# Float32 score operands over 128 partitions, batch 0's values loaded once, and a turn table in place of a planner

## The chip, the core and the metric

The kernel runs on one core of a Trainium2 chip. The metric is the device time of one execution in microseconds (us). A core has five engines that work side by side, each through its own list of instructions in a fixed order: TensorE (PE, matrix products; its weight loads are listed apart as PEld), VectorE (DVE), ScalarE (ACT), GpSimd (POOL) and SyncE (SP), which here issues every DMA. A transfer that SP issues is carried by the core's 16 DMA engines.

## The reference

Attention with a decay for 8 batches and 8 heads over 576 positions of width 64, and behind it a two-layer feed-forward net with the activation h·cos(h):

```python
scores = scale * np.matmul(q, k.transpose(0, 1, 3, 2))
cum = np.cumsum(np.log(np.clip(f, 0.0001, 1.0)), axis=-1)
scores = np.where(causal, -1000000000.0, scores + cum[:, :, :, None] - cum[:, :, None, :])
attn = np.exp(scores - scores.max(-1)); attn = attn / (attn.sum(-1) + 1e-09)
x = np.matmul(attn, v)            # -> 4608 tokens x 512
h = x @ w_in                      # 512 -> 2048
out = (h * np.cos(h)) @ w_out     # 2048 -> 512
```

## The kernel before

**Tiles and stages.** A unit of attention is a pair of heads, n = 0 to 31 (four to a batch); a unit of the net is half a batch's tokens, u = 0 to 15, of 320 or 256 tokens. For each pair the scores of a 128-row block come out of one or two matmuls (`mm`, into PSUM tiles pa1 and pa2), DVE adds the causal mask and takes the row maximum, ACT takes the exponential. `gemm1` (L1058) is the first layer: 12 matmuls for each 128 rows of h, float16 high and low parts; then DVE and ACT form h·cos(h) and split it into the two parts of g. `gemm2` (L1105) is the second layer.

**Three kinds of score operands.** Pairs 0 to 3 go through `attention32` (L764) and pairs 4 to 7 through `attention` with float32 operands too (NQ = 8): 16 heads. Their q and k lie in a tile "q32" of the ring `g` (pairs 0 to 3) or `stage` (pairs 4 to 7), filled by `load32` (L753): 64 partitions of q and k from DRAM (L759) and four partitions of decay sums from the DRAM tile `cum_d` (L760), so that a score matmul contracts over 68 partitions (L818, L973). From pair 8 on, scores are two matmuls of rounded parts (L975, L976).

**Weights.** W1 and W2 arrive as 64-bit words, 512 KB for each of 32 chunks (`stage`, L602; DMA at L627). DVE turns each chunk into float32 in three passes (L617, L621, L625), ACT takes a bound (L636). When all chunks of a column group are there, a scale is formed, and each chunk is split into float16 high (ACT, L646) and low (DVE, L653). W1's column group must be split before its `gemm1`, all of W2 before the first `gemm2`.

**Values.** `prep_vscale` (L705) loads the four value tiles of a batch into `stage` (L709) for a bound; the attention units load the same tiles again, into ring `v2` (L769 and L905).

**Buffers.** A ring is a set of buffers used in turn: `BUFS` gives their number (g 8, h 3, stage 2, v2 2). A tile waits until the last user of the tile that held its buffer is done.

**What sets the order.** All operations are recorded in a `Plan`, and `order` (L359) decides for each engine the order in which they are written. It runs a forward model of the engines with assumed costs, ranks by due times, runs it again, and then adds a hand-kept table `SHIFT` of time offsets. The model has a clock for TensorE (`Clock`, L222), and where it sees TensorE wait in the first 200 us (`FILL`) it writes filler matmuls on constant data ahead of the operation (`pads`, emitted at L1186), whose results are thrown away. Once written, each engine's order is fixed: an instruction that waits holds up all that stands behind it on its engine, SP's DMA issues included. Some operations have an alternative engine (`alt`): copies out of PSUM (ACT or DVE), the subtraction that makes g's low part (DVE L1101, or POOL L1102), the two subtractions behind the rounded q and k (L921, L922).

Of the kernel before, what the change touches and what calls it, by code (L numbers as in the profile page):

```python
# [24 lines left out]
P = 128  # L25
# [18 lines left out]
HOLDV, HOLDW, HOLDR, HOLDX = 0.0, 0.0, 25.0, 25.  # L44
NHP = 3
N32, NQ = 4, 8
ROUNDS = 2
AHEAD = 15
EARLY = 2
FILL, PAD = 200, 448  # L50
SWITCH = 6.0
TWO_PI = 2.0 * np.pi
NEG = -8.0e9
BUFS = dict(xs=1, stage=2, v2=2, vv=2, pt3=3, pt2=2, xh0=8, xl0=8, xh1=8, xl1=8, h=3, r=1, g=8, ot=1,
            pa2=1, pa1=3, hp=3, dg=1)

SHIFT = {
# [158 lines left out]
DMQ, DMC = int(1.35 * 360e3), int(0.5 * 360e3)  # L216
PADG, PADE, PE0 = 0.3, 0.0, 2.5
VACT = 2
T_DGE, T_DMA0, T_DMA1, DMA_BW, T_TABLE = 0.5, 0.65, 0.9, 360e3, 1.28


class Clock:  # L222
# [994 lines left out]
```

## Time and profile before

| | |
|---|---|
| time, 3 runs | median 1072.54 us (1072.24 to 1073.82) |
| the profiled execution's own time | 1073.1 us |
| its span, first to last instruction | 1071.4 us |
| mean granted TensorE clock | 0.992 |
| busy: PE, DVE, ACT, POOL | 1050.1, 819.7, 832.2, 155.3 us |
| filler matmuls | 158, 34.5 us of PE's busy time |
| DMA | 146.37 MB, mean 137 GB/s |

How to read it: "busy" of an engine is the union of its instructions' spans; filler matmuls count as PE's work in it. "Idle before" or "waited" is the time in which an engine had nothing running, put down to what ended it. "PEclk" is the share of full speed that TensorE's clock was granted. "DMA share" is the mean busy share of the 16 DMA engines, and a row of windows gives, for a stretch of the span, each engine's busy time (with its number of instructions), the clock, the DMA share and the rate.

### The profile page before, as it was taken

The numbers are of one execution on the slowest core, as the hardware profiler recorded it, in microseconds if no ns is written. First come the engines' busy times: TensorE is split into PE (matmuls) and PEld (weight loads), VectorE is DVE, ScalarE is ACT, GpSimd is POOL, SyncE is SP. The second block draws the span as 40 slices with busy tenths as digits, with TensorE's granted clock in tenths as the row PEclk, the third lists the DMA queues.
The fourth block names the chain that finished last, engine by engine and source line by source line (L and its number), as shares of the span: only waits on it lengthen the run. The fifth ranks groups of instructions, "written<-read, shape, count | busy, mean of one in ns | idle before, by whom it ended". The sixth has DMA issues, their size and how long they took to land. (4 is left out here: it accounts for less than half of the span.)

```text
span 1071.4 us, 23498 instructions
## 1 busy us (share of the span) xinstructions
PE 1050.1 (98%) x8975; PEld 841.6 (79%) x8975; DVE 819.7 (77%) x1801; ACT 832.2 (78%) x1739; POOL 155.3 (14%) x271
## 2 busy tenths in 40 slices
PE   8999999899999999999999999999999999999998
PEld 4778776688778887788778877778778877788787
DVE  6989999677887979678886879778776868671613
ACT  4758989588887989788888979887877978762522
POOL 1000000121121220221112211211211222000000
PEclk9999999799999999999999999999999999999999
DMA  8893463667767566647766667765776564430000
GB/s 267 309 284 109 99 135 102 126 162 158 180 152 147 139 142 167 149 101 159 182 154 144 127 148 167 169 129 130 178 144 144 134 142 75 85 59 21 7 20 20
DMA packets 256280, 146.37 MB, mean 137 GB/s; under 512 B 223337, under 2 KB 231529, under 8 KB 256169
## 3 DMA queue, kind: packets, MB, share of 16 engines
q1 hardware_dynamic: 256168, 144.88, 58.4%
q8 instruction: 70, 1.15, 0.5%
q14 instruction: 42, 0.34, 0.1%
HBM read 72.11 MB, written 10.62 MB: 77 GB/s over the span
## 5 line engine op out<-in xcount | busy, mean ns | idle before, releaser
L1118 PE MATMUL hp<-g,W2s 128*128 128x256 f16 (+1 forms) x3072 | 390.9, 287 | 0.6 <-DVE W2s L653 0.4
L1072 PE MATMUL hp<-xh,W1s 128*128 128x256 f16 (+1 forms) x2048 | 380.4, 286 | 1.1 <-ACT h L1078 1.1
L1118 PEld LDWEIGHTS <-W2s 128*128 128x128 f16 x3072 | 297.9, 98 | 78.0 <-issue 0.8
L1072 PEld LDWEIGHTS <-W1s 128*128 128x128 f16 x3072 | 295.9, 98 | 78.6 <-issue 1.7
L1072 PE MATMUL hp<-xl,W1s 128*128 128x256 f16 (+1 forms) x1024 | 292.6, 286 | 0.0
L1013 DVE SCALAR_TENSOR_TENSOR PS<-pa,ri,PS 128x576 f16<-128x576 f32 (+2 forms) x280 | 140.7, 544 | 32.1 <-ACT PS L1009 31.3
L992 ACT ACTIVATE pa<-pa,nb 128x576 f32<-128x576 f32 (+2 forms) x280 | 141.1, 506 | 19.8 <-DVE nb L987 18.6
L987 DVE CUSTOM_DVE_ANT_0 pa<-pa,mask 128x576 f32<-128x576 f32 (+2 forms) x280 | 131.5, 513 | 31.8 <-PE pa L976 26.1
L1009 ACT ACTIVATE PS<-pa,ri 128x576 f16<-128x576 f32 (+2 forms) x280 | 134.1, 545 | 15.0 <-DMA pt<-PS 9.7
L1078 ACT ACTIVATE h<-hp 128x320 f32<-128x320 f32 (+1 forms) x256 | 101.3, 416 | 36.6 <-PE hp L1072 36.0
L1093 DVE TENSOR_TENSOR h<-h,r 128x1280 f32<-128x1280 f32 (+1 forms) x64 | 89.1, 1392 | 41.4 <-ACT r L1091 41.2
L997 POOL TENSOR_SCALAR ri<-L 128x1 f32<-128x1 f32 (+1 forms) x168 | 46.8, 279 | 410.4 <-ACT pa L992 404.9
L921 POOL TENSOR_TENSOR QK<-stage,QK 64x576 fp32r<-64x576 f32 x46 | 77.3, 1680 | 170.5 <-issue 116.4
L1091 ACT ACTIVATE r<-r,halfpi,m_inv 128x1280 f32<-128x1280 f32 (+1 forms) x64 | 86.2, 1347 | 18.8 <-DVE r L1089 18.3
L1101 DVE TENSOR_TENSOR g<-h,g 128x1280 f16<-128x1280 f32 (+1 forms) x62 | 84.2, 1358 | 14.1 <-ACT g L1100 13.7
L1087 DVE TENSOR_SCALAR r<-h,m_a 128x1280 int32<-128x1280 f32 (+1 forms) x64 | 56.8, 888 | 49.3 <-ACT h L1078 48.3
L1089 DVE SCALAR_TENSOR_TENSOR r<-r,m_b,h 128x1280 f32<-128x1280 int32 (+1 forms) x64 | 91.3, 1426 | 0.7
L975 PE MATMUL pa<-QK 128*128 128x288 f32 (+4 forms) x288 | 90.3, 330 | 1.5 <-DVE PS L1013 1.5
L1100 ACT CAST g<-h 128x1280 f16<-128x1280 f32 (+1 forms) x64 | 74.2, 1159 | 15.1 <-DVE h L1093 14.9
L1124 ACT ACTIVATE ot<-hp,m_o 128x320 f32<-128x320 f32 (+1 forms) x64 | 32.3, 504 | 65.9 <-PE hp L1118 50.4
L1042 PEld LDWEIGHTS <-vv 128*64 128x64 f16 x1512 | 69.4, 111 | 16.9 <-issue 14.2
L1042 PE MATMUL pa<-pt,vv 128*64 128x256 f16 (+2 forms) x1512 | 78.8, 256 | 3.7 <-DMA pt<-PS 3.4
(118 smaller groups left out, 1166.7 us busy)
## 6 DMA issues: line engine op xcount, KB each, us to landing
stage<-in_dram SPq DMA_DIRECT2D x48, 576.0 KB
stage<-in_dram SPq DMA_DIRECT2D x32, 320.0 KB
v<-in_dram SPq DMA_DIRECT2D x32, 320.0 KB
g<-in_dram SPq DMA_DIRECT2D x16, 512.0 KB
h<-in_dram SPq DMA_DIRECT2D x16, 512.0 KB
QC<-QK SPq DMA_DIRECT2D x48, 144.0 KB
out_dram<-ot SPq DMA_DIRECT2D x32, 160.0 KB
out_dram<-ot SPq DMA_DIRECT2D x32, 128.0 KB
```

The source lines that it names most:

```text
L975: T.matmul(c, hi[:, 0, isl], hi[:, 1, d], start=True, stop=False)
L987: op("DVE", c_dve(w) + 0.008, lambda view=view, ib=ib, o=o, w=w, mk=mk, c=c: V.tensor_tensor_reduce(out=view(ib, o, w), in0=view(ib, o, w) ...
L992: op("ACT", c_act(w, True, 2), lambda view=view, ib=ib, o=o, w=w, c=c: A.activation(view(ib, o, w), view(ib, o, w), AF.Exp, bias=nb.get()[ ...
L1009: op("ACT", c_act(w, True, 1), lambda view=view, ib=ib, o=o, w=w, c=c, out_=out_: A.activation(out_(0), view(ib, o, w), AF.Copy, scale=ri. ...
L1013: op("DVE", c_dve(w) + 0.06, lambda view=view, ib=ib, o=o, w=w, c=c, out_=out_: V.scalar_tensor_tensor(out_(1), view(ib, o, w), ri.get()[: ...
L1042: T.matmul(d, vv.get()[:, jb, hd, kv], m, start=first and x == 0, stop=last and x == 2)
L1072: T.matmul(hp.get()[:, 0:w_], WS_[1][:, at(1, 4 * c + cb), w, fs], x.get(), start=(n == 0), stop=(n == 11))
L1078: op("ACT", c_act(w_, True), lambda hp=hp, k=k: A.activation(h.get()[:, k, 0:w_], hp.get()[:, 0:w_], AF.Copy, scale=float(2.0 ** -24)), re ...
L1089: op("DVE", c_dve(N) + 0.045, lambda: V.scalar_tensor_tensor(fl(r), fl(r).bitcast(I32), b1.get()[:, c:c + 1], fl(h), op0=ALU.mult, op1=ALU ...
L1091: op("ACT", c_act(N, aps=2), lambda: A.activation(fl(r), fl(r), AF.Sin, scale=inv.get()[:, c:c + 1], bias=halfpi), reads=[inv], writes=[r] ...
L1093: op("DVE", c_dve(N), lambda: V.tensor_tensor(fl(h), fl(h), fl(r), op=ALU.mult), reads=[r], writes=hk, prio=pr)
L1118: T.matmul(po.get()[:, 0:w_], WS_[2][:, at(2, 4 * c + k), w, msl], gh.get()[:, i, k, 0:w_], start=(n == 0), stop=(n == 47))
```

## The change

- **Operands.** A second input `qk2` holds q and k of the first 16 heads with 60 rows of zeros below the 64 of data: 124 rows. `load32` fills partitions 4 to 127 from it and partitions 0 to 3 with the decay sums, and the score matmuls of these heads contract over 128 partitions instead of 68. `qkT` keeps the other batches alone.
- **Values.** `load_v` keeps one tile per pair, and `prep_vscale(0)` reads that tile (ACT, junk output into ring `ot`): the values of batch 0 are loaded once. Ring v2 has 4 buffers instead of 2, ring g 7 instead of 8.
- **Order.** `rank`, `backward`, `shift` and `SHIFT` go. `TURN` lists all operations by number, and that place is the only key by which the model picks; `SWAP` names the operations that take their alternative engine. By the count of instructions in the order, POOL gets 36 of the 64 g subtractions (2 before), ACT 31 of 40 copies out of PSUM (25 before), and there are 115 filler matmuls (158 before), of which 75 stand ahead of the first score matmul (91 before) and 15 ahead of the first `gemm2` (none before). The model's constants change (DMA rate, clock thresholds, `FILL` 240), which counts only through the fillers.

```diff
-BUFS = dict(xs=1, stage=2, v2=2, vv=2, pt3=3, pt2=2, xh0=8, xl0=8, xh1=8, xl1=8, h=3, r=1, g=8, ot=1,
+BUFS = dict(xs=1, stage=2, v2=4, vv=2, pt3=3, pt2=2, xh0=8, xl0=8, xh1=8, xl1=8, h=3, r=1, g=7, ot=1,
...
+TURN = (
+    0, 6, 54, 30, 29, 1, 3, 74, 16, 7, 4, 8, 349, 59, 55, 56, 9, 57, 10, 58, 11, 12, 13, 75, 79, 76, 77, 18, 17, 78, 351, 350, 64, 60, 61,
...
     def order(self):
-        self.rank()
...
+        for k, i in enumerate(TURN):
+            o = self.ops[i]
+            o.due = k
+            if i in SWAP:
+                o.eng, o.cost, o.fn = o.alt[:3]
+        return self.forward()
...
-                    o = min(q, key=lambda x: (x.due - x.first + (switch if x.table not in (None, table) else 0.0), x.id))
+                    o = min(q, key=lambda x: x.due)
...
+    def load_v(n, pr):
+        if n not in V2:
+            b, p = divmod(n, NP)
+            v2 = V2[n] = ring("v2", [P, 5, P], F32)
+            op("SP", T_DGE, lambda: dma(v2.get(), vp[b, p].rearrange("p (j c) -> p j c", c=P)), writes=[v2], prio=pr, size=VSZ)
+        return V2[n]
...
+            if b == 0:
+                v2, jk = load_v(p, pr), ring("junk", [P, 640], BF16, tag="ot")
+                op("ACT", c_act(640, aps=1), lambda v2=v2, jk=jk, p=p: A.activation(
+                    jk.get(), v2.get().rearrange("p j c -> p (j c)"), AF.Square, accum_out=mx.get()[:, p:p + 1]),
+                   reads=[v2], writes=[mx.part(p), jk], prio=pr)
+                continue
...
-        op("POOL", 0.23, lambda: G.memset(q.get()[0:68, 0, 0:64], 0.0), writes=[q.part(0)], prio=pr - 1)
-        op("SP", T_DGE, lambda: dma(q.get()[0:64, :, ks], qkT[b, p, hd, 0:64]), writes=[q.part(1)], prio=pr - 1, size=DMQ)
-        op("SP", T_DGE, lambda: dma(q.get()[64:68, :, ks], cum_d[b * H + 2 * p + hd]),
+        op("POOL", 0.23, lambda: G.memset(q.get()[:, 0, 0:64], 0.0), writes=[q.part(0)], prio=pr - 1)
+        op("SP", T_DGE, lambda: dma(q.get()[4:P, :, ks], qk2[b, p, hd]), writes=[q.part(1)], prio=pr - 1, size=DMQ)
+        op("SP", T_DGE, lambda: dma(q.get()[0:4, :, ks], cum_d[b * H + 2 * p + hd]),
...
-                            T.matmul(c, qf.get()[0:68, 0, isl], qf.get()[0:68, 1, 64 + d.start:64 + d.stop], start=True, stop=True)
+                            T.matmul(c, qf.get()[:, 0, isl], qf.get()[:, 1, 64 + d.start:64 + d.stop], start=True, stop=True)
...
+    qk2 = np.zeros((nb, NP, 2, P - 4, 2, S), qk.dtype)
+    qk2[:, :, :, 0:D] = qk[:nb]
+    qkT = np.ascontiguousarray(np.concatenate([qk[nb:], qk[nb:]], axis=3))
```

SP's list, around the loads of q and k that follow the third head's (tiles g_582, g_586 and two of stage before; g_300 and two of stage now). L759 and L760 before are L774 and L775 now (q and k, decay sums); L627 is a chunk of weights (g_ for W2, h_ for W1). Before:

```order
L769 DMA v2_578<-in_1_dram 128x640
L760 DMA g_582<-cum_d_105 4x2x576
L759 DMA g_582<-in_0_dram 64x2x576
L627 DMA g_604<-in_4_dram 128x1024
L760 DMA stage_599<-cum_d_105 4x2x576
L759 DMA g_586<-in_0_dram 64x2x576
L627 DMA h_621<-in_3_dram 128x1024
```

Now:

```order
L627 DMA h_327<-in_4_dram 128x1024
L774 DMA g_300<-in_0_dram 124x2x576
L774 DMA stage_319<-in_0_dram 124x2x576
L774 DMA stage_309<-in_0_dram 124x2x576
L930 DMA QC0_82<-cum_d_105 4x2x576
L775 DMA stage_309<-cum_d_105 4x2x576
L627 DMA g_388<-in_5_dram 128x1024
L627 DMA h_397<-in_4_dram 128x1024
```

Three loads of 124 rows now stand one behind the other, two of them for pair 4, ahead of the twelfth weight chunk (g_388); before, weight chunks stood between them.

DVE's list, around the first mask of the sixth head (pa2_887 before; pa2_781 now, from tile g_678). L826 before is L839 now (mask and maximum), L617 to L625 the passes over a weight chunk, L894 before and L907 now the low part of x. Before:

```order
L617 TENSOR_SCALAR W1s_98<-h_817 128x512
L566 TENSOR_SCALAR dg_893<-eye_73,vm1_623 128x128
L894 SCALAR_TENSOR_TENSOR xl1_895<-hp_876,vs_471,xh1_890 128x256
L621 SCALAR_TENSOR_TENSOR W1s_98<-h_817,W1s_98 128x512
L826 ISA pa2_887,nb_730<-pa2_887,mask_66 128x2x288
L826 ISA nb_730 128x1
```

Now:

```order
L621 SCALAR_TENSOR_TENSOR W2s_99<-g_613,W2s_99 128x512
L907 SCALAR_TENSOR_TENSOR xl0_793<-hp_753,vs_351,xh0_770 128x320
L625 SCALAR_TENSOR_TENSOR W2s_99<-g_613,W2s_99 128x512
L839 ISA pa2_781,nb_652<-pa2_781,mask_66 128x2x288
L839 ISA nb_652 128x1
```

The mask stands behind fewer chunks of weights than before: three chunks' second and third passes have moved behind it.

More of the change, by code (lines that the diff above doesn't have):

```diff
@@ L43 @@
 LEAD = 2.5
-HOLDV, HOLDW, HOLDR, HOLDX = 0.0, 0.0, 25.0, 25.
+HOLDV, HOLDW, HOLDR = 0.0, 0.0, 25.0
 NHP = 3
 N32, NQ = 4, 8
-ROUNDS = 2
-AHEAD = 15
 EARLY = 2
-FILL, PAD = 200, 448
-SWITCH = 6.0
+FILL, PAD = 240, 448
 TWO_PI = 2.0 * np.pi
 NEG = -8.0e9
-BUFS = dict(xs=1, stage=2, v2=2, vv=2, pt3=3, pt2=2, xh0=8, xl0=8, xh1=8, xl1=8, h=3, r=1, g=8, ot=1,
+BUFS = dict(xs=1, stage=2, v2=4, vv=2, pt3=3, pt2=2, xh0=8, xl0=8, xh1=8, xl1=8, h=3, r=1, g=7, ot=1,
             pa2=1, pa1=3, hp=3, dg=1)
-SHIFT = {
[122 rows of a table removed]
-}
+TURN = (
[183 rows of a table added]
+)
+SWAP = {36, 43, 51, 50, 53, 116, 147, 473, 474, 569, 597, 663, 1005, 1004, 1206, 1207, 701, 1290, 1289, 1054, 1332, 1333, 1372, 1373, 1092,
[4 rows of a table added]
 class Buf:
@@ L207 @@
 class Op:
-    __slots__ = ("eng", "cost", "size", "table", "fn", "prio", "deps", "succ", "n", "ready", "id", "t", "alt", "due", "port", "first", "moving", "bank", "fill", "end", "pads", "hold")
+    __slots__ = ("eng", "cost", "size", "table", "fn", "prio", "deps", "succ", "n", "ready", "id", "t", "alt", "due", "port", "moving", "bank", "fill", "end", "pads", "hold")
 LAT = {("ACT", "ACT"): 0.034, ("ACT", "DVE"): 0.131, ("ACT", "PE"): 0.17, ("ACT", "POOL"): 0.18, ("ACT", "SP"): 0.13,
@@ L215 @@
 SHARED = {"DVE": "POOL", "POOL": "DVE"}
-DMQ, DMC = int(1.35 * 360e3), int(0.5 * 360e3)
+DMQ, DMC, VSZ = 8 * 124 * 576, int(0.4 * 410e3), 4 * P * 5 * P
 PADG, PADE, PE0 = 0.3, 0.0, 2.5
 VACT = 2
-T_DGE, T_DMA0, T_DMA1, DMA_BW, T_TABLE = 0.5, 0.65, 0.9, 360e3, 1.28
+T_DGE, T_DMA0, T_DMA1, DMA_BW, T_TABLE = 0.5, 0.65, 0.9, 410e3, 1.28
 class Clock:
-    W, HIGH, LOW, SLOW = 3.413, 0.49, 0.36, 2.0
+    W, HIGH, LOW, SLOW = 3.413, 0.36, 0.4, 2.0
     def __init__(self):
@@ L231, in close @@
         u = self.busy / self.W
-        self.warm = u > self.HIGH or (self.warm and u > self.LOW)
+        self.warm = u > (self.LOW if self.warm else self.HIGH)
         self.k, self.busy = self.k + 1, 0.0
@@ L254, in pad @@
             e = min(b, (self.k + 1) * self.W)
-            self.busy += (e - a) * (0.9 if self.warm else 0.5)
+            self.busy += (e - a) * (0.9 if self.warm else 0.45)
             n += (e - a) / ((1.0 if self.warm else 2.0) * (PAD / 2400 + 0.003))
@@ L264, in __init__ @@
     def __init__(self):
-        self.ops, self.rings, self.first = [], {}, 0.0
+        self.ops, self.rings = [], {}
     def ring(self, name, make):
@@ L278, in op @@
         o.eng, o.cost, o.size, o.table, o.fn, o.prio, o.alt, o.id = eng, cost, size, table, fn, prio, alt, len(self.ops)
-        o.port, o.first, o.moving, o.fill, o.pads, o.hold = port, self.first, moving, fill, 0, hold
+        o.port, o.moving, o.fill, o.pads, o.hold = port, moving, fill, 0, hold
         o.bank = []
@@ L310, in op @@
         return o
-    def rank(self):
-        t = 0.0
-        for o in self.ops:
-            o.due = 1e9
-        for o in sorted((o for o in self.ops if o.eng == "PE"), key=lambda o: (o.prio, o.id)):
-            o.due = t
-            t += o.cost
-        for o in reversed(self.ops):
-            c = T_DMA0 + o.size / DMA_BW + T_DMA1 if o.eng == "SP" else o.cost + 0.15
-            for x in o.succ:
-                o.due = min(o.due, x.due - c)
-    def backward(self, end):
-        free, avail, future, n = {}, {}, [], {}
-        late = {}
-        for o in self.ops:
-            free.setdefault(o.eng, 0.0)
-            avail.setdefault(o.eng, [])
-            n[o.id], late[o.id] = len(o.succ), 0.0
-            if not o.succ:
-                heapq.heappush(future, (0.0, o.id, o))
-        t, left = 0.0, len(self.ops)
-        while left:
-            while future and future[0][0] <= t + 1e-9:
-                o = heapq.heappop(future)[2]
-                heapq.heappush(avail[o.eng], (-end[o.id], o.id, o))
-            nxt = []
-            for e, q in avail.items():
-                if q and free[e] <= t + 1e-9:
-                    o = heapq.heappop(q)[2]
-                    left -= 1
-                    free[e] = t + o.cost
-                    stop = t + (T_DMA0 + o.cost + o.size / DMA_BW if e == "SP" else o.cost)
-                    o.due = -stop
-                    for d in o.deps:
-                        late[d.id] = max(late[d.id], stop + (T_DMA1 if d.eng == "SP" else LAT[d.eng, e]))
-                        n[d.id] -= 1
-                        if not n[d.id]:
-                            heapq.heappush(future, (late[d.id], d.id, d))
-                if q:
-                    nxt.append(free[e])
-            if future:
-                nxt.append(future[0][0])
-            t = max(t, min(nxt, default=t))
@@ L359, in order @@
-    def order(self):
-        self.rank()
-        base = [(o.eng, o.cost, o.fn) for o in self.ops]
-        for k in range(ROUNDS):
-            if k:
-                self.backward(end)
-            for o, x in zip(self.ops, base):
-                o.eng, o.cost, o.fn = x
-            out, end = self.forward()
-        self.shift()
-        return self.forward(0.0)[0]
-    def shift(self):
-        group = {}
-        for o in self.ops:
-            k = group.setdefault((o.fn.__code__.co_firstlineno, o.prio), o.id)
-            o.due, o.alt = o.t + o.first + SHIFT.get(k, 0.0), None
@@ L378, in forward @@
-    def forward(self, switch=SWITCH):
-        free, avail, future, out, ends = {}, {}, [], [], {}
+    def order(self):
+        for k, i in enumerate(TURN):
[4 more added lines that the diff above has]
+        return self.forward()
+    def forward(self):
+        free, avail, future, out = {}, {}, [], []
         for o in self.ops:
@@ L392, in forward @@
                 _, _, o = heapq.heappop(future)
-                if o.alt:
-                    def done(e, c):
-                        return max(t, free[e]) + c + sum(x.cost for x in avail[e] if x.due - x.first <= o.due - o.first)
-                    if done(o.alt[0], o.alt[1]) <= done(o.eng, o.cost) + o.alt[3]:
-                        o.eng, o.cost, o.fn = o.alt[:3]
                 avail[o.eng].append(o)
@@ L427, in forward @@
                     if e == "SP":
-                        dma_free = max(dma_free, t + min(o.cost, 0.625) + T_DMA0) + o.size / (DMA_BW if t > 10.0 else 0.6 * DMA_BW)
+                        dma_free = max(dma_free, t + min(o.cost, 0.625) + T_DMA0) + o.size / (DMA_BW if t > 5.0 else 0.6 * DMA_BW)
                         end = dma_free
@@ L432, in forward @@
                     span = max(span, end)
-                    ends[o.id] = o.end = end
+                    o.end = end
                     for s in o.succ:
@@ L445, in forward @@
         self.span = span
-        return out, ends
+        return out
 def c_dve(n, fast=False, k=1):
@@ L473, in fox_moe_kernel @@
 @with_exitstack
-def fox_moe_kernel(ctx: ExitStack, tc: tile.TileContext, qkT, vp, fT, w1, w2, out):
+def fox_moe_kernel(ctx: ExitStack, tc: tile.TileContext, qk2, qkT, vp, fT, w1, w2, out):
     nc = tc.nc
@@ L703, in fox_moe_kernel @@
     vs, ms = {}, {}
+    V2 = {}
+    def load_v(n, pr):
[4 more added lines that the diff above has]
+        return V2[n]
     def prep_vscale(b, pr):
@@ L767, in attention32 @@
         pr = float(n)
-        v2 = ring("v2", [P, 5, P], F32)
-        op("SP", T_DGE, lambda: dma(v2.get(), vp[b, p].rearrange("p (j c) -> p j c", c=P)), writes=[v2], prio=pr - 0.9,
-           size=4 * P * 5 * P, hold=HOLDX)
+        v2 = load_v(n, pr - 0.9)
         ks = slice(64, 64 + S)
@@ L790, in mm @@
                         o += 1
-            op("PE", 0.11 * nb_, mm, reads=reads, writes=[pm], prio=pr + 0.2, moving=0.48, fill=lambda: pm.get()[:, 0:PAD])
+            op("PE", 0.11 * nb_, mm, reads=reads, writes=[pm], prio=pr + 0.2, moving=0.9, fill=lambda: pm.get()[:, 0:PAD])
             o = 0
@@ L817, in mm @@
                         for c, d in ((d_[:, 0], slice(0, hf)), (d_[:, 1], slice(hf, S))) if big else ((d_, slice(0, w)),):
-                            T.matmul(c, qf.get()[0:68, 0, isl], qf.get()[0:68, 1, 64 + d.start:64 + d.stop], start=True, stop=True)
-                op("PE", 2 * c_mm4(S // 2) if big else sum(c_mm4(w) for _, _, w in blocks), mm, reads=xb, writes=[tb], prio=pr, fill=lambda tile_=tile_, big=big: tile_.get()[:, 0, 0:PAD] if big else tile_.get()[:, 0:PAD])
+                            T.matmul(c, qf.get()[:, 0, isl], qf.get()[:, 1, 64 + d.start:64 + d.stop], start=True, stop=True)
+                op("PE", 2 * c_mm4(S // 2) if big else sum(c_mm4(w) for _, _, w in blocks), mm, reads=xb, writes=[tb], prio=pr, moving=0.64, fill=lambda tile_=tile_, big=big: tile_.get()[:, 0, 0:PAD] if big else tile_.get()[:, 0:PAD])
                 for ib, o, w in blocks:
@@ L888, in turn_x @@
                     T.transpose(pm.get()[:, k * P:k * P + P], xs.get()[:, k].rearrange("p h d -> p (h d)"), eyef)
-            op("PE", 0.11 * m, turn_x, reads=[xs], writes=[pm], prio=pr + 0.6, moving=0.48, fill=lambda pm=pm: pm.get()[:, 0:PAD])
+            op("PE", 0.11 * m, turn_x, reads=[xs], writes=[pm], prio=pr + 0.6, moving=0.9, fill=lambda pm=pm: pm.get()[:, 0:PAD])
             xh, xl = ring(f"xh{half}", [P, w], F16), ring(f"xl{half}", [P, w], F16)
@@ L903, in attention @@
         pr = float(n)
-        v2 = ring("v2", [P, 5, P], F32)
-        op("SP", T_DGE, lambda: dma(v2.get(), vp[b, p].rearrange("p (j c) -> p j c", c=P)), writes=[v2], prio=pr - 0.9,
-           size=4 * P * 5 * P)
+        v2 = load_v(n, pr - 0.9)
         sets = [0, 0] if n < NQ else [next(turn) % NSET for hd in range(2)]
@@ L914, in prep @@
             qk = ring("stage", [P, 2, S], F32)
-            op("SP", T_DGE, lambda: dma(qk.get(), qkT[b, p, hd]), writes=[qk], prio=pr - 1, size=8 * P * S)
+            op("SP", T_DGE, lambda: dma(qk.get(), qkT[b - NQ // NP, p, hd]), writes=[qk], prio=pr - 1, size=8 * P * S)
             op("ACT", c_act(2 * S), lambda: A.copy(hi[:, :, ks], qk.get()), reads=[qk], writes=[x["hi"]], prio=pr)
@@ L972, in mm @@
                             if q32:
-                                T.matmul(c, q32.get()[0:68, 0, isl], q32.get()[0:68, 1, d], start=True, stop=True)
+                                T.matmul(c, q32.get()[:, 0, isl], q32.get()[:, 1, d], start=True, stop=True)
                                 continue
@@ L978, in attention @@
                 x2 = c_mm4 if q32 else lambda w: 2 * c_mmr(w)
-                op("PE", 2 * x2(S // 2) if big else sum(x2(w) for _, _, w in blocks), mm, reads=xb, writes=[tb], prio=pr, fill=lambda tile_=tile_, big=big: tile_.get()[:, 0, 0:PAD] if big else tile_.get()[:, 0:PAD])
+                op("PE", 2 * x2(S // 2) if big else sum(x2(w) for _, _, w in blocks), mm, reads=xb, writes=[tb], prio=pr, moving=0.64 if n < NQ else 1.0, fill=lambda tile_=tile_, big=big: tile_.get()[:, 0, 0:PAD] if big else tile_.get()[:, 0:PAD])
                 c0 = col
@@ L1146, in adv @@
         if n < len(gens):
-            pl_.first = AHEAD
             next(gens[n], None)
-            pl_.first = 0.0
     decay()
@@ L1195 @@
     qk = np.stack([x.transpose(0, 1, 3, 2).reshape(B, NP, 2, D, S) for x in (q, k)], axis=4)
-    qkT = np.ascontiguousarray(np.concatenate([qk, qk], axis=3))
+    nb = NQ // NP
+    qk2 = np.zeros((nb, NP, 2, P - 4, 2, S), qk.dtype)
+    qk2[:, :, :, 0:D] = qk[:nb]
+    qkT = np.ascontiguousarray(np.concatenate([qk[nb:], qk[nb:]], axis=3))
     vs = np.zeros((B, NP, 5 * P, P), v.dtype)
@@ L1202 @@
     ws = [w.view(np.int64) if w.dtype.itemsize == 8 else w for w in ws]
-    arrays = [qkT, vp, fT, *ws]
+    arrays = [qk2, qkT, vp, fT, *ws]
     nc = _bacc.Bacc("TRN2", target_bir_lowering=False, num_devices=1, dynamic_dma_scratch_size=1024)
```

308 rows, old and new, of tables (SHIFT, SWAP, TURN) are left out of this document.

## The prediction

> **What bounds the kernel now.** First the page's totals, then the windows by stage: up to the first `gemm1`, to the first weight chunk of W2 needed, to the first `gemm2`, and the rest.
>
> ```profile
> span 1071.4 us, 23498 instructions
> PE 1050.1 (98%) x8975; PEld 841.6 (79%) x8975; DVE 819.7 (77%) x1801; ACT 832.2 (78%) x1739; POOL 155.3 (14%) x271
> 0.00:114.30 114.30, 106.32 (x665) 79.13 (x666) 100.65 (x292) 77.15 (x220) 8.17 (x43) 0.99 0.74 229
> 114.30:166.80 52.50, 51.05 (x410) 38.18 (x409) 51.14 (x128) 48.09 (x102) 2.56 (x10) 1.00 0.54 115
> 166.80:204.30 37.50, 32.58 (x210) 21.95 (x208) 32.92 (x70) 29.39 (x61) 3.08 (x10) 0.82 0.54 133
> 204.30:1071.40 867.10, 860.13 (x7698) 702.36 (x7695) 634.99 (x1315) 677.58 (x1358) 141.45 (x209) 1.00 0.58 126
> ```
>
> Each row gives the stretch, its length, busy time (and number) of PE, PEld, DVE, ACT and POOL, the clock, the DMA share and GB/s. From 204.3 us on PE is busy 860.1 of 867.1 us: that stage is PE's own work, and the change does not touch it except through POOL. Time can be won or lost ahead of it. There "PE busy" misleads, since it holds the fillers (the second answer below counts them alone), and DVE has to be read in two halves:
>
> ```profile
> 0.00:114.30 114.30, 34.46 (x158) 15.93 (x158) 0.99 0.74 229
> 20.00:79.90 59.90, 55.18 (x344) 41.71 (x342) 55.18 (x159) 42.08 (x122) 1.00 (x7) 0.97 0.97 296
> 79.90:115.30 35.40, 34.43 (x245) 29.31 (x244) 34.88 (x116) 28.52 (x83) 2.31 (x12) 1.00 0.34 101
> ```
>
> Between 20 and 80 us the DMA engines are full (0.97); from 80 us to the first `gemm1` DVE is (34.88 of 35.40), with the DMA at 0.34. So the chain is: loads up to the sixth head's operands, then DVE, then PE. Its marks on the timeline (start, length, operation):
>
> ```profile
> 2.29 18.89 PE L1186 MATMUL pa<-mask,ones 128*128 128x448 bf16 x91 [2.29 <-POOL ones L497]
> 21.02 2.97 PE L818 MATMUL pa<-g 68*128 68x288 f32 x12
> 77.39 3.03 PE L818 MATMUL pa<-g 68*128 68x288 f32 x12
> 79.04 0.76 DVE L826 CUSTOM_DVE_ANT_0 pa<-pa,mask 128x576 f32<-128x576 f32 x1
> 114.29 0.43 PE L1072 MATMUL hp<-xh,W1s 128*128 128x320 f16 x2
> 114.95 0.48 DVE L894 SCALAR_TENSOR_TENSOR xl<-hp,vs,xh 128x256 f16<-128x256 f32 x1
> ```
>
> The sixth head's scores start at 77.39, its first mask at 79.04; from there DVE takes 35.9 us to its last low part of x ahead of `gemm1` (114.95), and `gemm1` starts at 114.29.
>
> **The new loads.** A load of q and k had 64 rows of partitions and now has 124. What that does depends on how many of the 16 engines carry it, and the trace can be asked, since every transfer ends with one 4-byte packet from each engine that took part. The first row below is a window with nothing but a 4-row load, the second one with only a 64-row copy, the third the whole span.
>
> ```profile
> DMA packets 12, 0.02 MB, mean 18 GB/s; under 512 B 4, under 2 KB 4, under 8 KB 12
> DMA packets 80, 0.15 MB, mean 134 GB/s; under 512 B 16, under 2 KB 16, under 8 KB 80
> DMA packets 256280, 146.37 MB, mean 137 GB/s; under 512 B 223337, under 2 KB 231529, under 8 KB 256169
> ```
>
> Four rows: 8 data packets and 4 small ones, so 4 engines. 64 rows: 64 and 16. For the writes of 56 rows to `cum_d` the whole span decides. Of 223,337 small packets, 112 transposes take 112×1,920 = 215,040 of 256 bytes; 8,297 are left. 273 transfers of 64 or 128 rows give 273×16 = 4,368, 64 of four rows 256, four of eight rows 32; the transposes, at 32 each (taken to be two sets of 16), 3,584. What remains is 57: four writes of 56 rows at 14, and one stray. At 16 each it would be 64. So 4 rows go on 4 engines, 56 on 14, 64 on 16: the largest number up to 16 that divides the rows. 124 is 4×31, so I read it as **4 engines**, and the other twelve idle through that load.
>
> [...]
>
> What an engine carries, from three windows: weight chunks alone, writes of 2,304-byte rows to `cum_d`, and a stretch of old 64-row loads.
>
> ```profile
> 9.50:10.50 1.00, 1.00 (x7) 0.54 (x6) 1.00 (x3) 0.07 (x1) 0.00 (x0) 1.00 1.03 422
> 27.85:28.35 0.50, 0.50 (x3) 0.26 (x2) 0.42 (x1) 0.50 (x3) 0.00 (x0) 1.00 1.03 380
> 71.50:73.50 2.00, 2.00 (x21) 2.00 (x19) 2.00 (x6) 1.26 (x4) 0.00 (x0) 1.00 1.03 197
> ```
>
> An old load is 64×2×2,304 = 295 KB; at 197 GB/s it takes 1.5 us of all engines. The new one is 571 KB. On 16 engines at 380 to 422 GB/s it takes 1.4 to 1.5 us, like the old one. On 4 engines, at a sixteenth of these rates each (23.8 to 26.4 GB/s), it takes 571/95 = 6.0 us (5.4 at the upper rate). I take 6.0, since its packets have the 2,304 bytes of the 380 row. [...]
>
> Now the sum for the four engines that all loads use. SP's list has, up to the load for the sixth head, nine loads of 124 rows, 26 weight chunks, 9 value loads and small ones. A chunk is 524 KB at 422 GB/s, 1.24 us, of which each engine has its sixteenth for that whole time; a value load 328 KB, 0.78 us. Start 2.3 (the timeline's first row) + 9×6.0 = 54.0 + 26×1.24 = 32.3 + 9×0.78 = 7.0 + small: the 4-, 8- and 56-row transfers, some 60 packets for each of the four at 2.3 KB/23.8 GB/s = 0.1 us, 6 = **101.6 us**. Before, that load landed at about 77.4. Scores to first mask is 1.65 us (77.39 to 79.04), so the mask comes at 103.3 instead of 79.04: 24 us late. DVE stands in its list behind it.
>
> From there DVE has its 35.9 us, and more, because the new list has moved weight work behind that mask: three more of L621, three of L625, one of L617 and two of L933 between the two marks.
>
> ```profile
> L621 DVE SCALAR_TENSOR_TENSOR W1s<-h,W1s 128x512 int32<-128x512 int32 x16 | 11.0, 687 | 0.1
> L625 DVE SCALAR_TENSOR_TENSOR W1s<-h,W1s 128x512 int32<-128x512 int32 x16 | 11.0, 687 | 0.1
> L617 DVE TENSOR_SCALAR W1s<-h 128x512 int32<-128x512 int32 x16 | 6.6, 421 | 1.2 <-DMA h<-in_dram 1.2
> L933 DVE SCALAR_TENSOR_TENSOR vv<-v,vs,vv 128x640 f16<-128x640 f32 x28 | 24.9, 889 | 2.3 <-ACT vv L931 2.3
> L1102 POOL TENSOR_TENSOR g<-h,g 128x1024 f16<-128x1024 f32 x2 | 4.3, 2135 | 18.7 <-ACT g L1100 18.7
> L1101 DVE TENSOR_TENSOR g<-h,g 128x1024 f16<-128x1024 f32 x30 | 36.7, 1223 | 8.1 <-ACT g L1100 7.9
> ```
>
> 6×0.69 + 0.42 + 2×0.89 = 6.3 us, say 6. 103.3 + 35.9 + 6 = 145 us for the last x, against 115: **+30 us**. Bounds: with 5.4 us a load (−5.4), the small packets half hidden between others (−3), and the moved DVE work fitting into its wait (−6), +15; nothing makes the loads faster than that on four engines. Upwards: SP's waits for buffers while the four engines idle, 5.
>
> **The other edits.** Contraction over 128 partitions instead of 68: a score matmul streams the same columns, no cost taken. No row shows a float32 matmul over 128 partitions; the first layer's over 128 are in another type. If it cost, it would be in PE, which has slack there. Zero rows: only bytes, counted above. Values once: four loads fewer, 3.1 us of DMA, counted in the nine. Fillers: 158 to 115 of 34.46/158 = 0.22 us; they fill waits and are gone from a path that now waits longer. Ring g with 7: a chunk of W2 waits earlier for a buffer; in the four-engine queue it waits anyway.
>
> After the first `gemm1`, PE has the same work. What it lost before: 1.45 us to 166.8, then 4.9 idle and (1−0.82)×37.5 = 6.75 in clock to 204.3, 11.7 in the last stretch. Of that, I give back 8: the list moves 34 subtractions for g from DVE to POOL, some ahead of the W2 splits that `gemm2` waits for, 1.22 us each on DVE (row L1101). Against it stand 15 fillers ahead of the first `gemm2`, 15×0.22 = 3.3, and pairs 5 to 7, whose 6 us loads come late, 2. Net −3 (bounds −11.7, +5). On POOL a subtraction takes 2.14 us (row L1102), 0.9 longer than on DVE; PE waits for g nowhere in the rows of before, so nothing is taken, and the range holds some of it.
>
> Sum: +30 − 3 = +27 on the profiled execution's 1073.1 (span 1071.4 and 1.7 around it) is 1100; the median of the runs lies 0.6 lower, so **1099 us**.
>
> **Rivals.** *A, spread over 16 (faster):* if the 124 rows go on all 16 engines, nine loads cost 13.5 us as before, no more slow stretch at 197 GB/s delays the chunks, and four value loads go. The sixth head's load would land by 2.3+13.5+32.3+7+6 = 61 us and not bind. Then the first scores come 16 fillers earlier (16×0.19 = 3.0 us, since they now start at the fillers' end), 8 come back before `gemm2`, 3 go to fillers: about −9, **1063 us**. For it: the 197 row shows what 64-row loads cost. Against it: 14 engines for 56 rows. Chance 0.10.
>
> *B, PE's clock falls too (slower still):* with DVE's chain late, PE waits in pieces, and after a wait the clock is down:
>
> ```profile
> 192.62 5.88 PE L973 MATMUL pa<-stage 68*128 68x448 f32 x12 [1.03 <-DMA stage<-in_dram]
> 210.63 2.97 PE L973 MATMUL pa<-stage 68*128 68x448 f32 x12
> ```
>
> The same twelve score matmuls take 5.88 and 2.97 us. PE has 34.4 us of work between the sixth head's scores and `gemm1` (row 79.90). DVE has 42 for that; as long as PE runs it at a mean clock over 34.4/42 = 0.82, DVE decides. At half clock it takes 69, 27 more than DVE: 1099 + 27 = **1126 us** at most, some 1112 at 0.62. Chance 0.11, most of it under 1127.
>
> *C, hidden or halved (no change):* the division is by the 248 DRAM rows, 8 engines: nine loads take 27 us, the sixth head's lands at 2.3+27+32.3+7+6 = 75, as now, and the gains and the 6 us on DVE cancel: **1072 us**. Against it: 56 rows of SBUF against more rows of DRAM went on 14. Chance 0.05.
>
> **How the numbers follow.** The forecast has 0.74: +15−11.7 gives 1076, +30+5+5 gives 1112. The range 1076 to 1127 holds it and most of B; A, C and the top of B are left out, under 0.2. A measurement can tell 0.2%, about 2 us: faster 0.11 (A and a little of C), same 0.04 (C), slower 0.85.
>
> **What would show it.** In the profile after: a window with nothing but a 124-row load shows 248 data packets, 4 small ones, a DMA share near 0.25 and about 95 GB/s; PE and DVE wait for g from DRAM for tens of us before the sixth head; its scores start near 102, the first `gemm1` near 145; from the first `gemm2` to the end the time is as before, within some us. Wrong would be: 16 small packets for such a load (A), 8 (C), the first `gemm1` before 120 us, or a loss that lies after 230 us (POOL's subtractions).

## The result, and the profile after

The changed kernel takes 1147.18 us (median of 4 runs, 1143.66 to 1149.74) against 1072.39 before (4 runs): 1.0692 times as long, interval 1.0662 to 1.0723. The sign was right and the size was not: +75 us instead of +27, above the range's 1127. The profiled execution took 1143.66.

The page's totals of the kernel after, and its windows up to the first `gemm1` (now at 171.70 us), to the first `gemm2`, and the rest:

```profile
span 1141.9 us, 23375 instructions
PE 1055.6 (92%) x8932; PEld 845.3 (74%) x8932; DVE 794.5 (70%) x1766; ACT 838.2 (73%) x1745; POOL 234.1 (20%) x300
0.00:171.70 171.70, 111.52 (x607) 83.41 (x608) 106.34 (x303) 81.84 (x233) 8.06 (x42) 0.81 0.57 168
171.70:233.70 62.00, 54.48 (x424) 39.54 (x423) 52.62 (x120) 53.61 (x107) 7.86 (x15) 1.00 0.58 113
233.70:1141.90 908.20, 889.62 (x7905) 722.30 (x7903) 635.51 (x1345) 702.77 (x1406) 218.16 (x244) 1.00 0.56 125
```

The first row is where the time went: 171.7 us to the first `gemm1` instead of 114.3, at a DMA share of 0.57 (0.74 before) and a clock of 0.81. From there to the end it is 970.2 us against 957.1. So 57.4 us were lost ahead of `gemm1` and 13.1 behind it, of 70.5 in the span.

The marks of the chain on the timeline: scores of the sixth head, its first mask, the first `gemm1`, the low part of x just behind its start; and the row of windows from that mask to `gemm1`.

```profile
126.56 5.42 PE L831 MATMUL pa<-g 128*128 128x288 f32 x16 [14.21 <-DMA g<-in_dram]
128.85 0.77 DVE L839 CUSTOM_DVE_ANT_0 pa<-pa,mask 128x576 f32<-128x576 f32 x1 [14.13 <-PE pa L831]
171.69 0.43 PE L1083 MATMUL hp<-xh,W1s 128*128 128x320 f16 x2
172.74 0.48 DVE L907 SCALAR_TENSOR_TENSOR xl<-hp,vs,xh 128x256 f16<-128x256 f32 x1
128.85:171.70 42.85, 41.11 (x291) 34.77 (x291) 40.33 (x133) 33.09 (x95) 2.27 (x12) 0.99 0.22 64
```

PE waited 14.2 us for that head's load alone, DVE for the scores behind it. From the first mask to the low part of x it is 43.9 us; the prediction had 42. DVE is busy for 40.3 of the 42.9 us to `gemm1` and PE for 41.1, at a clock of 0.99; which of the two sets the length, no run tells. What is off is when the mask comes: 128.85 instead of 103.3.

The number of engines can be seen directly. Between 48 and 54 us the kernel after moves almost nothing but loads of q and k; the count of packets in that window, and its row of windows:

```profile
DMA packets 261, 0.60 MB, mean 100 GB/s; under 512 B 4, under 2 KB 4, under 8 KB 260
48.00:54.00 6.00, 2.71 (x6) 1.75 (x7) 0.38 (x1) 1.24 (x7) 0.00 (x0) 0.75 0.26 100
```

Four small packets (4 bytes each in the trace), a share of 0.26 (four of sixteen), 100 GB/s. The prediction said 4, near 0.25 and about 95. Three such loads were issued between 40.06 and 47.3 us, and with more than one of them under way the share is still 0.26: they use the same four engines. The count over the whole span says it of all 16 loads:

```profile
DMA packets 257431, 149.48 MB, mean 131 GB/s; under 512 B 223080, under 2 KB 231272, under 8 KB 257320
```

Before there were 223,337 small packets, 257 more: 16 loads with 12 fewer each are 192, four value loads of 16 are 64, and one is a stray. With eight engines a load it would be 192, with sixteen 64.

But that is the load by itself. Four windows in which weight chunks are carried beside such a load (in the first also loads of values), and for comparison one with chunks alone; then the count of packets in the fourth:

```profile
8.00:14.00 6.00, 6.00 (x33) 3.13 (x32) 1.91 (x4) 0.72 (x2) 0.00 (x0) 1.00 1.06 218
56.00:62.00 6.00, 4.24 (x34) 3.98 (x34) 1.96 (x11) 4.03 (x14) 0.00 (x0) 0.94 1.00 246
84.00:92.00 8.00, 5.39 (x12) 3.61 (x13) 2.69 (x8) 0.72 (x2) 0.00 (x0) 0.50 1.02 264
114.00:124.00 10.00, 0.00 (x0) 0.00 (x0) 0.72 (x2) 1.24 (x5) 0.00 (x0) 0.59 1.05 229
68.00:70.00 2.00, 0.00 (x0) 0.00 (x0) 1.77 (x5) 0.00 (x0) 0.00 (x0) 0.51 0.99 395
DMA packets 714, 2.29 MB, mean 229 GB/s; under 512 B 52, under 2 KB 52, under 8 KB 714
```

The last two columns of a window are the DMA share and GB/s. In the first four all sixteen engines count as busy and move 218 to 264 GB/s; without such a load they move 395. From 114 to 124 us, PE does nothing at all. The 662 data packets of that window are of 2,304 bytes (the load) or 4,096 (chunks), and 2.29 MB make 236 of the one and 426 of the other. So the load moves 54 GB/s here, where alone it moves 100. The trace has a time for every packet: the load's take 178 ns on average in this window and 96 from 48 to 54 us, a chunk's 292 here and 163 from 68 to 70 us. Load and chunks slow each other here; the sum in the prediction gave each engine its full rate throughout.

### The profile page after: what moved, and what is told of

Same layout as the page of the kernel before. It is cut to its first block, busy times and chain, and to the rows that moved or that the text cites. A ratio compares the mean times of both kernels' runs of the same rounds, so it can differ in the third digit from the quotient of the medians.

```text
span 1141.9 us, 23375 instructions
## 1 busy us (share of the span) xinstructions
PE 1055.6 (92%) x8932; PEld 845.3 (74%) x8932; DVE 794.5 (70%) x1766; ACT 838.2 (73%) x1745; POOL 234.1 (20%) x300
## 5 line engine op out<-in xcount | busy, mean ns | idle before, releaser
L998 DVE CUSTOM_DVE_ANT_0 pa<-pa,mask 128x576 f32<-128x576 f32 (+3 forms) x280 | 132.4, 509 | 47.5 <-PE pa L987 37.4
L1008 POOL TENSOR_SCALAR ri<-L 128x1 f32<-128x1 f32 (+1 forms) x168 | 50.0, 298 | 352.0 <-ACT pa L1003 341.6
L1113 POOL TENSOR_TENSOR g<-h,g 128x1280 f16<-128x1280 f32 (+1 forms) x36 | 89.4, 2482 | 151.1 <-ACT g L1111 150.1
L1098 DVE TENSOR_SCALAR r<-h,m_a 128x1280 int32<-128x1280 f32 (+1 forms) x64 | 63.8, 997 | 54.5 <-ACT h L1089 53.3
L1100 DVE SCALAR_TENSOR_TENSOR r<-r,m_b,h 128x1280 f32<-128x1280 int32 (+1 forms) x64 | 98.7, 1542 | 0.9
L987 PE MATMUL pa<-QC 68*128 68x288 f32 (+4 forms) x288 | 76.5, 304 | 1.8 <-DMA QC<-QK 1.8
```

The lines of the kernel that those rows point to most:

```text
L987: T.matmul(c, co[0:68, 0, isl], co[0:68, 1, d], start=False, stop=True)
L998: op("DVE", c_dve(w) + 0.008, lambda view=view, ib=ib, o=o, w=w, mk=mk, c=c: V.tensor_tensor_reduce(out=view(ib, o, w), in0=view(ib, o, w) ...
L1100: op("DVE", c_dve(N) + 0.045, lambda: V.scalar_tensor_tensor(fl(r), fl(r).bitcast(I32), b1.get()[:, c:c + 1], fl(h), op0=ALU.mult, op1=ALU ...
L1113: alt=("POOL", 0.9 * c_pool(N), lambda: G.tensor_tensor(gx(1), fl(h), gx(0), op=ALU.subtract), SLG))
```

## The experiments

**Theory 1:** the four engines are the cause. **Theory 2:** the new order is, whose SP list waits for value buffers ahead of loads that are due (SP's longest waits, 43.9 us in three, up to 180 us). In each run the lists of PE, DVE and ACT are those of the kernel it starts from, except where it is said.

### Operands and order apart: a_split, a_64, b_124, b_split

Run a_split, in the changed kernel (b_split has the same in the kernel before):

```
-        ... dma(q.get()[4:P, :, ks], qk2[b, p, hd])
+            dma(q.get()[4:116, :, ks], qk2[b, p, hd, 0:112])
+            dma(q.get()[116:P, :, ks], qk2[b, p, hd, 112:124])
```

Run a_64 puts the old 64 rows (partitions 4 to 67, contraction over 68) into the changed kernel; b_124 puts the 124 rows into the kernel before.

> The changed kernel, but each load of 124 rows is issued as one of 112 rows and one of 12 (by the division that the trace of before showed: 16 and 12 engines); the order on PE, DVE, ACT and POOL is unchanged. Theory 1, the four engines: the loss of 75 us goes, 1063 to 1080 us, first gemm1 before 125 us, and SP's waits for value buffers (43.9 us in three) shrink to under 15, since they only followed from late heads. Theory 2, the new order with its value loads ahead of the loads of q and k on SP: the long waits stay, 1120 us or more. Theory 3, half each: 1095 to 1115.

> The changed kernel with 64 rows a load and 68 partitions a score matmul as before (no zero rows), in the new order. Theory 1: 1065 to 1085 us, with the slow stretches of about 200 GB/s during these loads as in the kernel before. Theory 2: 1120 us or more. If zero rows over 128 partitions help the DMA, this is slower than the split version by some us; if not, it is equal or faster.

> The kernel before, in its own order, with the operands of the change alone (124 rows, decay sums in partitions 0 to 3, 128 partitions). Theory 1: slower by 25 to 60 us, 1098 to 1132, with 4 small packets and about 100 GB/s during a lone load. Theory 2: 1070 to 1078 us.

> The kernel before in its own order with the operands of the change, loaded as 112 and 12 rows. Theory 1: within 6 us of before, either side: no loss without the four engines; the stretches of 200 GB/s gone if they came from 64 partitions being written. Theory 2: the same, so it tells only what the 128 partitions are worth: 1064 to 1078 us.

| run | order | loads | us | ratio to before | first gemm1 |
|---|---|---|---|---|---|
| after | new | 124 rows | 1147.18 | 1.0692 (1.0662 to 1.0723) | 171.7 |
| b_124 | old | 124 rows | 1139.48 | 1.0610 (1.0573 to 1.0647) | 175.3 |
| a_split | new | 112 and 12 | 1088.95 | 1.0147 (1.0114 to 1.0181) | 128.1 |
| b_split | old | 112 and 12 | 1082.16 | 1.0070 (1.0038 to 1.0103) | 123.8 |
| a_64 | new | 64 rows | 1090.15 | 1.0146 (1.0097 to 1.0195) | 121.4 |

None of the four lies in the range that its text gives for theory 1: b_124 lost more than 60 us, and the other three are 8 to 16 us slower than the kernel before. Still theory 1 holds for the greater part: with the same bytes and the same order, splitting the load takes away 58 us in the new order and 57 in the old one. In a_split SP still waits 28.0 us in three for value buffers, not under 15, and the loss goes all the same. Theory 2 holds for a rest: with the old loads the new order is still 1.5% (some 15 us) slower; with the loads of 124 rows, whole or split, it costs 7 to 8 us (a_split against b_split, after against b_124). A surprise is b_split: with all engines at work the operands still cost 0.7%, where rival A expected a gain. A window of it that holds almost nothing but such loads:

```profile
64.00:67.00 3.00, 2.98 (x19) 1.98 (x18) 2.86 (x11) 1.34 (x7) 0.00 (x0) 1.00 1.07 238
```

238 GB/s on sixteen engines: 571 KB take 2.4 us, not the 1.4 to 1.5 of the prediction. An old load of 295 KB took 1.5.

### The count of engines as a dose: a_7eng

As a_split, but 119 and 5 rows; 119 is 7×17.

> The changed kernel with each load of 124 rows issued as 119 and 5 rows: 119 is 7 times 17, so 7 engines if the count is a divisor of the rows. If the loss of 58 us between the split version (1089) and the changed kernel (1147) goes with the packets that the busiest engine carries (16, 34 and 62 of 93 ns for 16, 7 and 4 engines): 1089 + 58 x 18/46 = 1112 us, 1100 to 1124. If a threshold decides (the chain is hidden until it exceeds another): under 1098. If the count is not a divisor and 119 rows go on 16: 1089.

1116.35 us, 1.0408 (1.0375 to 1.0440). A window with almost only such loads:

```profile
42.00:46.00 4.00, 0.60 (x1) 0.50 (x2) 0.75 (x6) 2.13 (x10) 0.00 (x0) 0.57 0.46 168
```

A share of 0.46 is 7.4 engines. The time lies 4 us from the line between 16 and 4 engines, so with these three counts the loss goes with the packets of the busiest engine, and no threshold shows. That line is 58 us for 46 packets of 93 ns (4.3 us a load): 13.5 us lost for each us that a load is longer. The prediction's sum had nine loads count.

### SP's waits: a_v6g6

```
-v2=4 ... g=7
+v2=6 ... g=6
```

> The changed kernel with its four-engine loads, but 6 value buffers and 6 g buffers (4 and 7): SP's waits for a value buffer, 43.9 us in three, should go. If these waits lengthen the chain: 1120 to 1138 us instead of 1147. If they only follow from late heads: 1142 to 1152.

1143.09 us, 1.0672 (1.0633 to 1.0710), with small changes in all lists. SP's waits up to 180 us, the first line in the kernel after, the other two here (total, times, longest):

```profile
SPq L711 <- PE hp L876: 43.9, 3, 19.5
SPq L711 <- PE hp L876: 12.9, 2, 12.3
SPq L775 <- PE hp L802: 15.4, 1, 15.4
```

The waits for a value buffer behind PE fell from 43.9 to 12.9 us, and the time by 4, inside the two intervals; the first `gemm1` comes at 172.07. As far as this run goes (it also takes a buffer from g), value buffers are not what makes the heads late. But SP hardly stands less: it waits elsewhere, as at a load of decay sums (15.4 us, in the kernel after 6.4), and all its waits up to 180 us add up to 107.5 against 114.5. That a waiting SP costs nothing is not shown.

### What of the order costs: a_64_dve

Every subtraction for g is emitted on DVE at POOL's place in the sequence:

```
+                on_dve = o.fn
                 o.eng, o.cost, o.fn = o.alt[:3]
+                if o.alt[0] == "POOL" and o.alt[3] == SLG:
+                    o.fn = on_dve
```

> The changed kernel with 64 rows a load (1090 us), and every subtraction for g emitted on DVE at the place in the sequence where POOL had it; the lists of PE, ACT and SP are the same. If the 8 us that the new order loses between the first gemm2 and 600 us come from g on POOL (2.5 us against 1.3 on DVE): 1078 to 1084 us. If they come from the order of the other work (PE waiting for the transposes and for DVE's PS): 1087 to 1093, or slower, since DVE has 45 us more work.

1090.29 us, 1.0158 (1.0105 to 1.0211): as a_64. Against DVE, POOL's subtractions, which the prediction left at nothing, cost nothing that this run sees. The order's own loss is visible in a_64 in two places, its first 65.6 us and a stretch in which it does the PE work that the kernel before does from 240 to 600 us (360 us):

```profile
0.00:65.60 65.60, 50.13 (x240) 35.04 (x241) 51.59 (x134) 36.64 (x105) 5.75 (x30) 0.84 0.89 285
245.00:613.00 368.00, 360.75 (x3243) 294.03 (x3242) 277.22 (x603) 314.16 (x628) 113.10 (x118) 1.00 0.65 146
PE hp L569 <- DVE dg L566: 7.1, 1, 7.1
PE pa L1053 <- DMA pt<-PS: 3.0, 4, 1.0
PE pa L986 <- DVE PS L1024: 3.0, 4, 1.2
```

The waits are PE's (total, times, longest), the first of the early stretch, the others of the late one. Early, the matmul for the scale of the values stands right behind the first head's scores and waits 7.1 us, and the clock is 0.84 where the kernel before had 0.97 in its first 60 us. Late, PE loses 7 us in pieces to transposes and to PS. Both are seen in the trace; neither was taken away in a run. The profiled execution of a_64 took 1082.70 us, the shortest of four (the longest 1094.05), so its trace shows the smaller part of the loss.

### Why sixteen engines are slow: b_pad, b_pad64, b_vsrc

All three start from the kernel before. b_pad and b_pad64 have rows of 640 columns in DRAM, so that a partition's bytes are one run (112 and 12 rows; 64 rows). b_vsrc reads the 64 rows from the array of v, so the scores of these heads are made of other data and only its time and rates count:

```
-        dma(q.get()[0:64, :, ks], qkT[b, p, hd, 0:64])
+        dma(q.get()[0:64, :, ks], vp[b, p].rearrange("(d t) c -> d t c", t=2)[:, :, 0:S])
```

> The kernel before in its own order with the 124-row operands as 112 and 12 rows, but rows of 640 columns in DRAM (64 zeros ahead of each), so that a partition's 5,120 bytes are one run. If the row shape (2,304 bytes at an offset of 256) is what holds these loads at 255 GB/s: near 400 GB/s, 1.5 us a load, and 1064 to 1075 us. If it is the partitions or the source, the rate stays near 250 and the time near b_split's 1082, with 11% more bytes up to 1086.

> The kernel before, 64 rows a load, rows of 640 columns in DRAM as above. If 64 partitions are what holds the old loads at 200 GB/s, still 200 and 1072 to 1077 us. If the row shape does, 400 GB/s, and 1064 to 1074 us.

> The kernel before, its 64-row loads taken from the array of v instead of that of q and k (same rows, same packets; the scores of the first 16 heads are then computed from other data, the rest is unchanged). If the source holds those loads at 200 GB/s: near 400 now. If the 64 partitions that are written do: 200, as before. Time 1070 to 1076 either way.

1082.43 (1.0089, 1.0069 to 1.0110), 1073.52 (1.0014, 0.9992 to 1.0037) and 1071.86 us (1.0008, 0.9987 to 1.0028). Stretches with many of these loads, in that order (in the first, a third of the bytes are chunks'):

```profile
62.00:64.00 2.00, 2.00 (x10) 1.40 (x9) 1.45 (x5) 0.69 (x2) 0.00 (x0) 1.00 1.06 221
```

```profile
60.00:62.00 2.00, 1.98 (x15) 1.26 (x13) 1.97 (x9) 1.89 (x7) 0.00 (x0) 1.00 1.04 209
```

```profile
57.00:59.00 2.00, 1.99 (x15) 1.21 (x13) 2.00 (x8) 1.34 (x5) 0.00 (x0) 1.00 1.06 206
```

Neither the shape of a row nor, for 64 rows, the source array matters. Of the causes thought of, where the rows are written is left.

### Which partitions: b_128, a_128, b_120, a_120, b_own, b_ports

b_128 and a_128 load all 128 rows at once and then write the decay sums over the first four. b_120 and a_120 load 120 rows into partitions 8 to 127, b_own 120 rows into 0 to 119, each with a load of 4 zero rows; in b_own the decay sums go to 120 to 123. b_ports moves no zeros:

```
+            dma(q.get()[0:32, :, ks], qkT[b, p, hd, 0:32])
+            dma(q.get()[64:96, :, ks], qkT[b, p, hd, 32:64])
```

> The kernel before in its own order, operands of 128 partitions loaded as 128 rows in one transfer (four zero rows at the top, over which the decay sums are then written). 8 partitions for each of 16 engines, as weight chunks have. If it is the count of partitions for an engine (4 with 64 rows, 7 with 112) that holds those loads at 200 and 255 GB/s: near 400 GB/s, 1.5 us a load, and 1068 to 1076 us. If it is the source: near 255, and 1080 to 1085 as with 112 and 12 rows.

> The changed kernel with the same loads of 128 rows in one transfer. By partitions for an engine: faster than the split version (1089), 1078 to 1086, since the order's own loss (some 10 to 15 us with 64 rows) stays. By source: 1086 to 1092.

> The kernel before in its own order, operands over 128 partitions, loaded as 120 rows into partitions 8 to 127 (15 engines of 8 partitions) and 4 rows of zeros; nothing is overwritten, so SP has no new wait. If whole groups of 8 partitions are what lets a load run at full rate: 380 to 400 GB/s, 1.5 us a load, no slowed chunks, and 1064 to 1074 us. If only the full 128 rows do: near 250 GB/s and 1078 to 1086.

> The changed kernel with the same loads. By groups of 8 partitions: 1074 to 1084, below the 1089 of the split into 112 and 12 rows, and what stays above the kernel before is the order's own. Otherwise 1086 to 1092.

> The kernel before in its own order, 120 rows into partitions 0 to 119 (15 engines, 8 partitions each, not shifted), 4 rows of zeros at the end, the decay sums in 120 to 123. If the shift by one group slowed the 120-row load: 380 to 400 GB/s and 1066 to 1076 us. If the engines' groups of 8 neighbours collide in any case, and only the 128-row split is free of it: 200 to 250 GB/s and 1080 to 1088.

> The kernel before in its own order, with the 64 rows as two loads of 32, into partitions 0 to 31 and 64 to 95, zeros in 32 to 63 by POOL, decay sums in 96 to 99, so a score matmul contracts over 100 partitions. [...]

| run | us | ratio to before |
|---|---|---|
| b_128 | 1090.61 | 1.0181 (1.0140 to 1.0221) |
| a_128 | 1095.32 | 1.0222 (1.0181 to 1.0263) |
| b_120 | 1086.96 | 1.0115 (1.0079 to 1.0151) |
| a_120 | 1094.25 | 1.0197 (1.0154 to 1.0240) |
| b_own | 1085.76 | 1.0125 (1.0093 to 1.0157) |
| b_ports | 1073.10 | 1.0003 (0.9981 to 1.0025) |

Stretches full of these loads, of b_128, b_120, b_own and b_ports in that order:

```profile
68.00:70.00 2.00, 1.98 (x13) 1.15 (x13) 2.00 (x11) 1.08 (x5) 0.00 (x0) 1.00 1.02 392
```

```profile
65.00:69.00 4.00, 2.60 (x15) 1.72 (x15) 2.79 (x8) 3.18 (x11) 0.00 (x0) 1.00 1.04 223
```

```profile
63.00:66.00 3.00, 3.00 (x20) 1.89 (x19) 2.96 (x11) 2.24 (x8) 0.00 (x0) 0.98 1.00 224
```

```profile
59.00:61.00 2.00, 1.98 (x15) 1.26 (x14) 2.00 (x9) 1.50 (x6) 0.00 (x0) 1.00 0.88 222
```

Only the load of all 128 partitions ran about as fast as chunks alone (395 GB/s in the kernel after): at 392, three of them and a chunk side by side. 120 rows, shifted by one group of 8 or not, ran at 223 and 224; my idea that each engine needs a group of 8 to itself fell with b_own. Yet b_128 and a_128 are slower than either of their ranges (a_120 is too, by 2 us). In b_128 the decay sums wait for the load to land, and SP stands still for that; I take this for the reason, but no run took the wait away. SP's longest wait up to 130 us in b_128:

```profile
SPq L759 <- DMA g<-in_dram: 33.0, 7, 7.1
```

b_ports writes as many rows as the kernel before, spread over both halves of the partitions: 222 GB/s against 197, and the time is the same. Why 64, 112 and 120 rows stay at 197 to 238 GB/s at DMA shares of 1.00 to 1.07, and 128 do not, no run shows: these rates are measured here and not explained. a_128 and a_120 lie 5 and 7 us above b_128 and b_120: the order's own loss comes on top. No version beat the kernel before; b_ports equals it.

## Why the prediction was right or wrong

- **Four engines for 124 rows: right**, by the packets (4 in the window, 257 fewer in all) and by a_7eng (7.4 engines for 119). The cause of most of the loss is that: 57 to 58 us in either order.
- **6.0 us a load: right alone, wrong in company.** Alone, a load moves 100 GB/s (5.7 us). The step that failed is the term 9×6.0 = 54 us, with "a sixteenth of these rates each": beside chunks the load's packets take 178 ns, not 96, and all engines together move 218 to 264 GB/s. The eighth and ninth load, which stand ahead of the sixth head, have their packets between 107.1 and 125.9 us: 18.7 us and not 12. From 56 us to that head's scores, the 1,293 packets of this size (five loads and small ones) took 46.9 us on four engines; at 93 ns they would have taken 30.1. That is 17 us, an estimate, of the 25 by which the scores came behind the sum (126.6 against 101.6). The other 8 are not settled: the chunk packets on the same four engines are slowed too, and SP waits, and no run separates these.
- **42 us from the first mask to the last x: right within 2 us**, 43.9; 42.8 to the first `gemm1`.
- **The clock (rival B): there, but not the cause.** It fell to 0.81 ahead of `gemm1`, in the waits (0.59 from 114 to 124 us, where PE does nothing). Once the sixth head's scores were there it was 0.99, and the stretch took about what the forecast gave it.
- **Net −3 behind `gemm1`: wrong**, it was +13. PE's work is the same (943.8 us busy before, 944.1 now); its idle time went from 13.3 to 26.1 us. The 8 us that I gave back did not come. PE's longest waits behind `gemm1` now:

```profile
PE hp L1083 <- ACT h L1089: 5.6, 5, 2.3
PE pa L1053 <- DMA pt<-PS: 5.0, 5, 2.0
PE pa L984 <- DMA stage<-cum_d: 4.1, 1, 4.1
```

  The first two were 1.1 and 3.4 us before. The third is a late pair's decay sums. In the profiled executions the part behind `gemm1` is 7.2 us longer than before in b_124 (new loads, old order) and 2.5 in a_64 (old loads, new order), and in b_124 a single wait for a late pair's load takes 7.8 us (1.0 before). So the late pairs, priced at 2, seem to be more of it than the order. That the order waits for transposes and PS in the steady stage, which I had taken for unchanged, a_64 shows too: 7 us in the stretch above.
- **POOL's subtractions at nothing: right** (a_64_dve). **Contraction over 128 partitions at nothing: right**: twelve score matmuls of a_split take 2.97 us where before they took 2.97.

```profile
35.12 2.97 PE L835 MATMUL pa<-g 128*128 128x288 f32 x12
```

- **Rival A: wrong in its price.** Without the four engines the operands lose 0.7%; 112 rows run at 238 GB/s, not at 380. **Rival C: out**; its 248 rows are the 124 of q and the 124 of k, and there are 257 fewer small packets where eight engines would give 192.

In sum: 30 was 57 ahead of `gemm1`, −3 was +13 behind it. The forecast's +27 had its sign from a mechanism that was there, and its size from taking the rate of a load from windows in which it would be alone, and from leaving out the waits of the new order behind `gemm1`.

## What to carry to other kernels

Before rows are added to a DMA, count the engines that it will use: here the small packets of the profile told it, and 124 rows ran on 4 engines of 16, at 100 GB/s alone, where 128 rows ran at 392 with the DMA engines full (a share of 1.02). Price a slow transfer in the company in which it will run: here it was slowed itself, from 100 to 54 GB/s, and slowed the chunks beside it, from 163 to 292 ns a packet. And look at what a faster load makes wait: in b_128, whose loads ran at 392 GB/s, SP stood 33.0 us in seven waits for loads into whose rows it writes a second time, and the time was 1090.61 us.

## What the runs showed of the hardware that was not expected

- A four-engine load and weight chunks beside it slowed each other to about half: the load from 100 to 54 GB/s, a chunk's packets from 163 to 292 ns, all sixteen engines together to 229 GB/s (chunks alone 395). Why is open.
- The rate of a load went with the partitions written: 197 GB/s for 64 rows (206 from the array of v, 209 with padded rows), 238 for 112, 223 and 224 for 120, 392 for 128. One run of 5,120 bytes a partition instead of two of 2,304 did not raise it (221 for 112 rows, 209 for 64).
- Two loads of 32 rows, one into each half of the partitions, reached 222 GB/s where one of 64 rows into the lower half ran at 197, and left the time as it was (1073.10 us, 1.0003).
